# Attention and routed experts on one core: a tile's bias rows loaded by halves, two GpSimd steps made full height

## The chip, the cores and the metric

One core of a Trainium2 chip runs the whole program in one launch. The metric is the device time of one execution in microseconds, taken as the median over runs. The kernel before takes 859.41 us (three runs, 858.2 to 860.89).

## The reference

Causal attention with a learned decay feeds a top-1 mixture of experts.

```python
# q, k, v: (8, 8, 576, 64), s: (8, 8, 576)
scores = q @ k.T / sqrt(64)
cum    = cumsum(maximum(s, 0), -1)
bias   = minimum(-(cum[:, None] - cum[None, :]), 0)      # per row and column
scores = where(causal, -1e9, scores + bias)
attn   = softmax(scores) @ v                             # (8, 8, 576, 64)
x      = attn as 4608 tokens of 512
e      = argmax(x @ w_gate); g = softmax weight of e     # 8 experts
out    = g * (relu(x @ w1[e]) @ w2[e])                   # 512 -> 1024 -> 512
```

Everything is float32. The kernel computes each product from a rounded high part and a low part (high times high, high times low, low times high).

## The kernel before

**Pairs and tiles.** The 64 heads are worked in 32 pairs. A pair's queries and keys lie with one head on partitions 0 to 63 and the other on 64 to 127. The 576 query rows are four tiles of 128 for each head (g = 0 to 3), and the last 64 rows of both heads together form the *mixed* tile (g = 4, `MIX`), whose rows 0 to 63 belong to the first head and 64 to 127 to the second.

**Bias.** The row part of the bias cancels in the softmax, so only a column bias is needed. It is computed once, scaled by 8, and written to a DRAM tensor `bias` of 64 x 576. For each pair `load_b` (LB, L142) brings the first 512 columns of both heads, repeated on all 128 partitions, and `load_c` (LC, L148) brings the mixed tile's `bx`: the first head's 576 values repeated on partitions 0 to 63 and the second head's on 64 to 127. Both are issued from SyncE's queue. `causal` (M0, M2, M3, M4, L152) puts -8e9 above the diagonal, on GpSimd; M4 does the last 64 columns of `bx`, one half of the partitions at a time.

**The split.** `split` (L188) makes the high and low parts: K0 on VectorE, K1 (low part of q, into `h`) and K3 (low part of k, `kl`) on GpSimd, and K4, which copies the last 64 query columns into `qd`, a tile with one 64 x 64 block per head on its diagonal and zeros off it. K4 is two copies, one per half of the partitions. There are two `qd` tiles, used in turn, and their zeros are written at the start on ScalarE.

**The steps of a pair.** TensorE computes the scores (S0 to S3; S4 and SM are the two parts of the mixed tile, of which the first product needs `qd` and the second `kl`), transposes the exponentials (T0 to T4) and multiplies with v (AV). VectorE adds the bias and takes the row maximum (Z0 to Z4, L276), ScalarE takes the exponential (X0 to X4, L290) and moves the transposes out (C0 to C4, L320). Every four pairs form a batch of 576 tokens, whose routing (RA to RD and others; eight steps on TensorE) is spread over later pairs. Its rows are scattered by expert into a DRAM tensor `xs` by GpSimd's indirect transfers (SD, L462).

**What sets the order.** `ORDER` is a list per engine, written by hand; "+n" is how many pairs a step lags. `loop` walks the lists and emits each step as soon as the steps that it needs are emitted, so every engine runs its list strictly in order. What the change touches:

```python
"POOL": "M0+1 K1+0 M2+1 K4+0 M4+0 K3+0 SD+0 M3+0",
"SP": "PASS+3 LB+2 LV+4 LX+0 LC+1",
```

PASS is a step on SyncE that waits for S4 of its pair; SM waits for it, and so do the transfers behind it in SyncE's queue. By the lags, LC of pair p stands behind PASS of pair p-2. There are two buffers of `bx`, two of `b`, two of `kl`.

**After the attention** the experts run one after the other on the sorted tokens (L846 to L1060): two layers, with the rows written to the output by GpSimd's indirect transfers (L896).

Of the kernel before, what the change touches and what calls it, by code (L numbers as in the profile page):

```python
# [8 lines left out]
F32 = mybir.dt.float32  # L9
# [4 lines left out]
AF = mybir.ActivationFunctionType  # L14
ALU = mybir.AluOpType
# [4 lines left out]
P, HP = 128, 64  # L20
B, H, S, D = 8, 8, 576, 64
# [10 lines left out]
BIG = -8.0e9  # L32
# [44 lines left out]
class Attention:  # L77
    def __init__(self, ctx, tc, K, qkv, s, rt, ps_t, dr):
        self.tc, self.nc, self.K, self.qkv, self.rt, self.ps_t = tc, tc.nc, K, qkv, rt, ps_t
        nc = tc.nc  # L80
        pool = lambda name, bufs: ctx.enter_context(tc.tile_pool(name=name, bufs=bufs))
        self.ldx, c2, c0, self.lq, self.ld, self.ldv = (
            pool("a_x", 3), pool("a_c2", 1), pool("a_c0", 1), pool("a_q", 2), pool("a_k", 2), pool("a_v", 4),
        )
        self.wk, c1, cp, self.sm = pool("a_wk", ZB), pool("a_c1", 1), pool("a_c", 1), pool("a_sm", 10)
        self.lb, self.lc = pool("a_b", NB), pool("a_bx", NB)
        self.qd = [c2.tile([P, 2, 2, HP], F32R, name=f"qd{i}") for i in range(2)]
        self.Es = [c1.tile([P, 2, w], F32, name=f"E{g}") for g, w in enumerate(TW[:4])]
        self.Es.append(c1.tile([P, 640], F32, name="E4"))
        self.aT = [(c0, cp)[i].tile([P, 5, 2, S], F32, name=f"aT{i}") for i in range(2)]  # L90
        self.ps_s = ctx.enter_context(tc.tile_pool(name="ps_s", bufs=2, space=PSUM))
        self.st = {}
        self.open = True

        flat = self.aT[1].rearrange("p a h c -> p (a h c)")
        raw, cum, zz, rows = (flat[:, S * i : S * i + S] for i in range(4))
        self.bias = dr.tile([B * H, S], F32, name="bias")
        keep = tc.keep_in_program_order
        keep(nc.vector.memset(zz, 0.0))
        self.queue(nc.sync.dma_start(raw[: B * H], s))  # L100
        self.load(0)
        self.load(1)
        for i in range(2):
            nc.scalar.activation(
                self.qd[i].rearrange("p a h c -> p (a h c)"), zz[:, : 4 * HP], AF.Copy
            )
        self.split(0, 0)
        r = slice(0, B * H)
        keep(nc.vector.tensor_scalar(out=raw[r], in0=raw[r], scalar1=0.0, scalar2=None, op0=ALU.max))
        keep(nc.vector.tensor_tensor_scan(  # L110
            out=cum[r], data0=raw[r], data1=zz[r], initial=0.0, op0=ALU.add, op1=ALU.add
        ))
        keep(nc.vector.tensor_scalar(
            out=rows[r], in0=cum[r], scalar1=cum[r, S // 2 : S // 2 + 1], scalar2=8.0, op0=ALU.subtract, op1=ALU.mult
        ))
        for part in (1, 3):
            keep(self.split(0, part))
        self.split(0, 4)
        self.rows = rows[r]

        warm = self.ps_s.tile([P, 2, 512], F32, name="s")[:, 0]
        zb = zz.bitcast(BF16)
        for x in range(WARM):
            for c in ((0, 256), (256, 512)) if x % 3 == 0 else ((0, 512),):
                nc.tensor.matmul(
                    warm[:, c[0] : c[1]], zb[:, :P], zb[:, P + c[0] : P + c[1]],
                    start=True, stop=True, skip_group_check=True,
                )
        nc.gpsimd.memset(self.Es[MIX][:, S:], 0.0)
        self.LT = rt.tile([P, 640], F32, name="LT", bufs=1)  # L130
        nc.gpsimd.memset(self.LT[:, S:], 0.0)
        self.xb, self.sums, self.sumx, self.rr, self.ra = [], [], [], [], []
        for i in range(2):
            self.xb.append(rt.tile([P, 4, 640], F32, name=f"xb{i}", bufs=1))
            nc.gpsimd.memset(self.xb[i][:, :, S:], 0.0)
            self.sums.append(rt.tile([P, 4, 8], F32, name=f"sums{i}", bufs=1))
            self.sumx.append(rt.tile([P, 4], F32, name=f"sumx{i}", bufs=1))
            self.rr.append(rt.tile([P, 5, 8], F32, name=f"rr{i}", bufs=1))
            nc.gpsimd.memset(self.rr[i][:, 4], 1.0)
            self.ra.append(rt.tile([P, 2, 5, 4], F32, name=f"ra{i}", bufs=1))  # L140
# [6 lines left out]

    def load_c(self, p):  # L148
        x = self.st.setdefault(p, {})["c"] = self.lc.tile([P, S], F32, name="bx")
        self.queue(self.nc.sync.dma_start(x, self.bias[2 * p : 2 * p + 2].unsqueeze(1).broadcast_to([2, 64, S])))  # L150

    def causal(self, p, part):  # L152
        aff = lambda out, x, pattern: self.nc.gpsimd.affine_select(  # L153
            out=out, in_=x, pattern=pattern, compare_op=ALU.is_ge, fill=BIG, base=0, channel_multiplier=1
        )
        b = self.st[p]["b"]
        if part == 0:
            cut = lambda x: x.rearrange("p h (k c) -> p h k c", c=P)
            aff(cut(b[:, :, 512:]), cut(b[:, :, :256]), [[0, 2], [0, 2], [-1, P]])
        elif part in (2, 3):  # L160
            x = b[:, :, P * part : P * part + P]
            aff(x, x, [[0, 2], [-1, P]])
        else:
            for h in range(2):
                x = self.st[p]["c"][64 * h : 64 * h + 64, 512:]
                aff(x, x, [[-1, 64]])

    def load(self, p):
        x = self.ldx.tile([P, 2 * S], F32, name="qk")
# [18 lines left out]
    def split(self, p, part):  # L188
        nc = self.nc
        d = self.st[p]  # L190
        q, k = d["x"][:, :S], d["x"][:, S:]
        if part == 0:
            d["h"] = self.lq.tile([P, 3, S], F32R, name="h")
            d["kl"] = self.ld.tile([P, S], F32R, name="kl")
            if p:
                nc.vector.tensor_copy(d["h"][:, :2].rearrange("p a c -> p (a c)"), d["x"])
            else:
                for i, x in enumerate((q, k)):
                    nc.scalar.activation(d["h"][:, i], x, AF.Copy)
        elif part in (1, 3):  # L200
            x, hi, lo = (q, d["h"][:, 0], d["h"][:, 2]) if part == 1 else (k, d["h"][:, 1], d["kl"])
            e = nc.gpsimd if p else nc.vector
            return e.tensor_tensor(out=lo, in0=x, in1=hi.bitcast(F32), op=ALU.subtract)  # L203
        else:
            for h in range(2):
                r = slice(64 * h, 64 * h + 64)
                nc.gpsimd.tensor_copy(self.qd[p % 2][r, :, h], d["h"][r, ::2, 512:].bitcast(F32))

    def mms(self, groups, first=True, last=True):
        for n in range(len(groups[0][1])):  # L210
# [970 lines left out]
```

## Time and profile before

| what | value |
|---|---|
| median of three runs | 859.41 us (858.2 to 860.89) |
| the profiled execution | 861.1 us, its span 859.4 us |
| TensorE products busy | 768.7 us, 89% |
| weight loads busy | 616.9 us, 72% |
| VectorE busy | 448.1 us, 52% |
| ScalarE busy | 426.5 us, 50% |
| GpSimd busy | 262.2 us, 31% |
| mean granted TensorE clock | 0.945 of full speed |
| transfers | 131.59 MB, mean 153 GB/s |

The profile is of one execution. PE is TensorE (PEld its weight loads), DVE VectorE, ACT ScalarE, POOL GpSimd, SP SyncE; a q behind a name is that engine's queue of issued transfers. L153 is line 153 of the kernel. "out<-in" gives an operation's tiles by their names in the program. Where an engine sat idle before an operation, the bracket gives how long and what released it; a wait for several things is put down to the one that came last. TensorE's times are modelled at their ends, so its busy share is not a measure of its use. GpSimd's are rough.

### The profile page before, as it was taken

How to read it: one execution, taken by the hardware profiler on the slowest of the kernel's cores; microseconds unless marked ns; L12 is line 12 of the kernel's file. 1: busy time of each engine (PE TensorE's matmuls, PEld its weight loads, DVE VectorE, ACT ScalarE, POOL GpSimd, SP SyncE). 2: the span in 40 equal slices, each digit the busy share in tenths (PEclk: the TensorE clock that was granted, in tenths of full speed). 3: DMA queues.
4: the chain of work that ended last, by engine and by line, in shares of the span. 5: the costliest groups of instructions: out<-in, count | busy, mean ns of one | idle time of the engine just before them, and what ended most of it. 6: DMA issues, size and time to landing. Idle time of an engine off the chain costs nothing.

```text
span 859.4 us, 18213 instructions
## 1 busy us (share of the span) xinstructions
PE 768.7 (89%) x6948; PEld 616.9 (72%) x6948; DVE 448.1 (52%) x1188; ACT 426.5 (50%) x1029; POOL 262.2 (31%) x407
## 2 busy tenths in 40 slices
PE   5487879798888797977999999999999999999987
PEld 3375767686777675755688888888788888887876
DVE  3345666666686575765651736354255255442611
ACT  1566878777787695855241515242243234331510
POOL 2444545555665656554200010101010010000001
PEclk8578999989999998989999999999999999999999
DMA  6666545556565565454670727263054045360201
GB/s 179 209 200 204 163 145 164 197 170 210 169 210 170 182 198 153 152 171 147 227 247 25 250 88 257 88 211 119 14 192 155 14 161 190 109 223 29 68 15 50
DMA packets 56746, 131.59 MB, mean 153 GB/s; under 512 B 4527, under 2 KB 4527, under 8 KB 56624
## 3 DMA queue, kind: packets, MB, share of 16 engines
q1 hardware_dynamic: 48240, 106.34, 38.4%
q0 software_dynamic: 5936, 18.92, 6.0%
q10 hardware_dynamic: 2448, 4.74, 1.5%
q8 instruction: 73, 1.20, 0.6%
q14 instruction: 49, 0.40, 0.1%
HBM read 101.97 MB, written 28.27 MB: 152 GB/s over the span
## 4 chain that ended last, share of the span: by engine, by line
PE 42%; issue 28%; DMA 13%; POOL 7%; DVE 5%; ACT 2%; POOLq 1%; SPq 1%; another core or an unknown queue 0%; DVEq 0%
PE ph L859 13%; DMA xs<-xr,dsi 8%; PE py L889 8%; PE s L212 6%; PE t L330 5%; PE t L294 3%; DVE z L276 3%; PE ph L889 3%; POOL kl L203 2%; DMA qk<-in_qkv_dram 2%; POOL bx L153 1%; ACT E L290 1%; ACT aT L320 1%; POOL out_dram L896 1%; DMA out_dram<-y,xr 1%
## 5 line engine op out<-in xcount | busy, mean ns | idle before, releaser
L859 PE MATMUL ph<-xT,w1t 128*128 128x512 f32 x768 | 181.0, 393 | 4.3 <-DVE xT L769 2.2
L290 ACT ACTIVATE E<-z,m 128x128 f32<-128x128 f32 (+4 forms) x288 | 166.0, 579 | 36.4 <-PE t L294 14.5
L859 PEld LDWEIGHTS ph<-xT,w1t 128*128 128x128 f32 x768 | 143.8, 189 | 37.7 <-DVE xT L769 2.6
L896 POOL DMA_INDIRECT out_dram<-y,xr x39 | 37.7, 966 | 390.6 <-DVE y L895 315.2
L320 ACT COPY aT<-t 128x512 f32<-128x512 f32 (+4 forms) x160 | 108.7, 685 | 78.9 <-PE t L294 77.2
L889 PE MATMUL py<-w2t,hT 128*128 128x512 f32 x552 | 130.6, 392 | 0.0
L889 PEld LDWEIGHTS py<-w2t,hT 128*128 128x128 f32 x552 | 102.5, 188 | 21.4
L276 DVE CUSTOM_DVE_ANT_0 z<-s,b 128x512 f32<-128x512 f32 (+2 forms) x192 | 91.2, 509 | 20.9 <-POOL b L153 6.3
L212 PE MATMUL s<-h 64*128 64x256 f32 (+3 forms) x512 | 98.8, 391 | 0.9 <-DVE xr L451 0.7
L330 PE MATMUL t<-aT,v 128*64 128x64 f32 (+2 forms) x1408 | 98.5, 297 | 0.6 <-ACT aT L320 0.6
L294 PEld LDWEIGHTS t<-ident,E 64*128 64x128 f32 x1600 | 76.9, 154 | 25.1 <-ACT E L290 8.8
L861 ACT ACTIVATE hT<-ph 128x512 fp32r<-128x512 f32 x64 | 37.7, 595 | 112.5 <-PE ph L859 110.7
L294 PE MATMUL t<-ident,E 64*128 64x64 f32 x1600 | 86.6, 243 | 3.3 <-ACT aT L320 3.3
L330 PEld LDWEIGHTS t<-aT,v 128*64 128x64 f32 x1408 | 69.0, 141 | 20.3 <-ACT E L290 2.8
L864 DVE SCALAR_TENSOR_TENSOR hT<-ph,hT 128x512 fp32r<-128x512 f32 x64 | 43.7, 689 | 47.2 <-ACT hT L861 46.5
L212 PE MATMUL s<-kl,qd 64*128 64x288 f32 (+1 forms) x124 | 24.7, 384 | 48.0 <-POOL kl L203 48.0
L212 PE MATMUL s<-h,qd 64*128 64x288 f32 (+1 forms) x248 | 50.1, 378 | 13.5 <-SPq L599 7.7
L276 DVE CUSTOM_DVE_ANT_0 z<-s,bx 128x576 f32<-128x576 f32 x32 | 24.2, 756 | 71.6 <-PE s L212 31.8
L212 PEld LDWEIGHTS s<-h 64*128 64x128 f32 x512 | 57.6, 222 | 4.5 <-DVE m L276 0.9
L153 POOL TENSOR_SCALAR_AFFINE_SELECT b<-b 128x256 f32<-128x256 f32 (+1 forms) x96 | 49.1, 528 | 25.8 <-DVE m L276 24.2
L889 PE MATMUL ph<-w2t,hT 128*128 128x512 f32 x216 | 53.8, 402 | 2.2 <-issue 2.2
L895 DVE TENSOR_SCALAR y<-py,xr 128x512 f32<-128x512 f32 x26 | 19.5, 750 | 69.3 <-PE py L889 69.3
(151 smaller groups left out, 1067.6 us busy)
## 6 DMA issues: line engine op xcount, KB each, us to landing
raw<-in_w_dram SPq DMA_DIRECT2D x32, 1024.0 KB, 7.0
qk<-in_qkv_dram SPq DMA_DIRECT2D x32, 576.0 KB, 11.8
b<-bias SPq DMA_DIRECT2D x32, 512.0 KB, 9.2
v<-in_qkv_dram SPq DMA_DIRECT2D x32, 320.0 KB, 9.8
bx<-bias SPq DMA_DIRECT2D x32, 288.0 KB
xr<-xs SPq DMA_DIRECT2D x8, 1028.0 KB
xs<-blank ACTq DMA_DIRECT2D x9, 514.0 KB, 8.1
xs<-blank SPq DMA_DIRECT2D x8, 514.0 KB
```

The costliest lines, as they stand in the source:

```text
L153: aff = lambda out, x, pattern: self.nc.gpsimd.affine_select(out=out, in_=x, pattern=pattern, compare_op=ALU.is_ge, fill=BIG, base=0, chan ...
L212: ins = self.nc.tensor.matmul(out, terms[n][0], terms[n][1], start=first and n == 0, stop=last and n == len(terms) - 1, skip_group_check=True,
L276: ins = nc.vector.tensor_tensor_reduce(out=cut(z[:, :w]), in0=x, in1=bias, scale=-0.125, scalar=3.0e38, op0=ALU.add, op1=ALU.min, accum_out=m,
L290: nc.scalar.activation(out, z[:, :w], AF.Exp, bias=m, scale=-1.0, accum_out=total)
L294: self.nc.tensor.transpose(out, src[r], self.K["ident"][r, r])
L320: return self.nc.scalar.copy(o, i)
L330: nc.tensor.matmul(ps[64 * h : 64 * h + 64, bank, lo - 512 * bank : hi - 512 * bank], v[:, kt, h], self.aT[p % 2][:, kt, h, lo:hi], start= ...
L859: nc.tensor.matmul(ps, w[:, a, d, c], x[:, b, d], start=n == 0, stop=n == 11)
L861: ins = nc.scalar.activation(h[:, 0, f], ps, AF.Relu)
L864: nc.vector.scalar_tensor_tensor(out=h[:, 1, f], in0=ps, scalar=0.0, in1=h[:, 0, f].bitcast(F32), op0=ALU.max, op1=ALU.subtract)
L889: self.nc.tensor.matmul(ps, hT[:, a, f, c], w[:, b, f % 4], start=f == 0 and i == 0, stop=f == 7 and i == 2)
L896: disjoint(self.tc, "out", self.nc.gpsimd.indirect_dma_start(out=self.out, out_offset=IndirectOffsetOnAxis(ap=row[:, DM + 1 : DM + 2].bitc ...
```

## The change

The mixed tile's bias rows come in two transfers of 64 partitions instead of one of 128 whose source has an outermost dimension of 2. K4 becomes one multiply on all 128 partitions: the query columns, repeated for both diagonal places, times `half`, which is 1 on a head's own block and 0 on the other, so that the zeros are written anew each time and need no preparation. M4 becomes one addition of `last`, which holds 0 up to the diagonal and -8e9 above it in each half. `half` and `last` are made once at the start on GpSimd, and the two ScalarE operations that wrote the zeros of `qd` go.

```diff
+        self.half = c2.tile([P, 2, HP], F32, name="half")
...
-        for i in range(2):
-            nc.scalar.activation(
-                self.qd[i].rearrange("p a h c -> p (a h c)"), zz[:, : 4 * HP], AF.Copy
+        self.last = c2.tile([P, HP], F32, name="last")
+        nc.gpsimd.memset(self.last, 0.0)
+        for h in range(2):
+            x = self.last[64 * h : 64 * h + 64]
+            nc.gpsimd.affine_select(
+                out=x, in_=x, pattern=[[-1, HP]], compare_op=ALU.is_ge, fill=BIG, base=0, channel_multiplier=1
             )
+        nc.gpsimd.memset(self.half, 0.0)
+        for h in range(2):
+            nc.gpsimd.memset(self.half[64 * h : 64 * h + 64, h], 1.0)
...
-        self.queue(self.nc.sync.dma_start(x, self.bias[2 * p : 2 * p + 2].unsqueeze(1).broadcast_to([2, 64, S])))
+        for h in range(2):
+            self.queue(self.nc.sync.dma_start(
+                x[64 * h : 64 * h + 64], self.bias[2 * p + h : 2 * p + h + 1].broadcast_to([64, S])
+            ))
...
-            for h in range(2):
-                x = self.st[p]["c"][64 * h : 64 * h + 64, 512:]
-                aff(x, x, [[-1, 64]])
+            x = self.st[p]["c"][:, 512:]
+            self.nc.gpsimd.tensor_tensor(out=x, in0=x, in1=self.last, op=ALU.add)
...
-            for h in range(2):
-                r = slice(64 * h, 64 * h + 64)
-                nc.gpsimd.tensor_copy(self.qd[p % 2][r, :, h], d["h"][r, ::2, 512:].bitcast(F32))
+            nc.gpsimd.tensor_tensor(
+                out=self.qd[p % 2], in0=d["h"][:, ::2, 512:].bitcast(F32).unsqueeze(2).broadcast_to([P, 2, 2, HP]),
+                in1=self.half.unsqueeze(1).broadcast_to([P, 2, 2, HP]), op=ALU.mult,
+            )
```

## Rows read from the trace of the kernel before

**Rows 1.** Busy time by stretch (from:to, length), granted clock, DMA share, GB/s.
```profile
core 0: us, PE busy (x) PEld busy (x) DVE busy (x) ACT busy (x) POOL busy (x), PEclk, DMA share, GB/s
...
18.00:400.00 382.00, 314.30 (x4653) 254.08 (x4653) 238.81 (x834) 274.52 (x750) 209.05 (x339) 0.89 0.58 183
...
146.00:352.00 206.00, 174.32 (x2668) 142.23 (x2670) 139.04 (x484) 155.85 (x427) 124.55 (x193) 0.93 0.58 183
226.00:246.00 20.00, 19.92 (x338) 16.03 (x333) 15.98 (x57) 19.08 (x57) 11.27 (x19) 1.00 0.62 198
```

**Rows 2.** Waits in 18 to 400: total us, times, longest us.
```profile
PE s L212 <- POOL kl L203: 48.0, 24, 5.1
...
PE s L212 <- POOL qd L207: 4.7, 4, 1.5
...
POOL bx L153 <- DMA bx<-bias: 65.2, 19, 6.6
POOL qd L207 <- DMA xs<-xr,dsi: 44.4, 14, 5.0
```

**Rows 3.** Order of time: issues and masks of bx (start, us; idle before).
```profile
8.52 0.64 SPq L150 DMA_DIRECT2D bx<-bias  x1
...
106.71 0.50 SPq L150 DMA_DIRECT2D bx<-bias  x1
...
17.11 0.53 POOL L153 TENSOR_SCALAR_AFFINE_SELECT bx<-bx 64x64 f32<-64x64 f32 x2 [7.69 <-DMA bx<-bias]
...
123.48 0.52 POOL L153 TENSOR_SCALAR_AFFINE_SELECT bx<-bx 64x64 f32<-64x64 f32 x2 [3.94 <-DMA bx<-bias]
```

**Rows 4.** A stretch within the first bx transfer: busy times, then packets.
```profile
14.30:15.90 1.60, 0.00 (x0) 0.00 (x0) 0.00 (x0) 0.00 (x0) 0.00 (x0) 0.53 0.13 50
...
DMA packets 35, 0.08 MB, mean 50 GB/s; under 512 B 0, under 2 KB 0, under 8 KB 35
```

**Rows 5.** GpSimd in order of time.
```profile
27.17 1.40 POOL L203 TENSOR_TENSOR kl<-qk,h 128x576 fp32r<-128x576 f32 x1
...
149.07 0.97 POOL L462 DMA_INDIRECT xs<-xr,dsi  x1 [0.30 <-issue]
150.04 1.02 POOL L153 TENSOR_SCALAR_AFFINE_SELECT b<-b 128x256 f32<-128x256 f32 x2
...
152.75 0.28 POOL L207 CAST qd<-h 64x128 fp32r<-64x128 f32 x1
156.72 0.29 POOL L207 CAST qd<-h 64x128 fp32r<-64x128 f32 x1 [3.69 <-DMA xs<-xr,dsi]
...
350.38 1.41 POOL L203 TENSOR_TENSOR kl<-qk,h 128x576 fp32r<-128x576 f32 x1
...
367.38 1.41 POOL L203 TENSOR_TENSOR kl<-qk,h 128x576 fp32r<-128x576 f32 x1
```

**Rows 6.** The chain that ended last, its first step: the load of s.
```profile
0.82 2.87 DMA aT<-in_s_dram
```

**Rows 7.** GpSimd's operations by line and shape, 18 to 420: busy, mean ns.
```profile
L203 POOL TENSOR_TENSOR h<-qk,h 128x576 fp32r<-128x576 f32 x31 | 44.0, 1419 | 11.0 <-PE s L212 6.4 <-PE t L294 2.4 <-DVE h L196 2.1
...
L207 POOL CAST qd<-h 64x128 fp32r<-64x128 f32 x62 | 18.7, 301 | 45.4 <-DMA xs<-xr,dsi 44.4
...
L153 POOL TENSOR_SCALAR_AFFINE_SELECT bx<-bx 64x64 f32<-64x64 f32 x62 | 15.8, 256 | 67.5 <-DMA bx<-bias 65.2
...
L791 POOL TENSOR_TENSOR w1t<-raw,w1t 128x512 fp32r<-128x512 f32 x4 | 5.0, 1278 | 0.0
```

**Rows 8.** TensorE in order of time: the mixed tile's products.
```profile
159.59 0.40 PE L212 MATMUL s<-kl,qd 64*128 64x288 f32 x2 [2.13 <-POOL kl L203]
...
227.87 0.38 PE L212 MATMUL s<-h,qd 64*128 64x288 f32 x2
...
237.21 0.40 PE L212 MATMUL s<-h,qd 64*128 64x288 f32 x2
...
245.71 0.40 PE L212 MATMUL s<-h,qd 64*128 64x288 f32 x2
```

## The prediction, as put on record before the result was known

> **What bounds the kernel now.** I read the page's engine shares first, then the busy times by stretch, the waits of TensorE and GpSimd, GpSimd's work and SyncE's queue in order of time, and last a stretch in which TensorE doesn't wait.
>
> The change touches only the attention, which ends near 400 us. There no engine is full: TensorE is busy 314.30 of 382 us, ScalarE 274.52, GpSimd 209.05, at a granted TensorE clock of 0.89 [rows 1]. So the attention is held by waits. TensorE's largest is 48.0 us in 24 waits for `kl`, which GpSimd makes at L203 (K3); 4.7 us go to `qd` [rows 2]. GpSimd is free nearly half of the time, but late: it waits 65.2 us before the mixed tile's mask (L153, M4) for the `bx` transfer and 44.4 us before a `qd` cast (L207, K4), put down to scatters into `xs` [rows 2]. In its queue stand K4, M4, K3: whatever holds the first two holds `kl`, and TensorE with it.
>
> The first stall: `bx` lands late because it moves slowly. The k-th pair of masks belongs to the k-th transfer. The first was issued at 8.52 and its masks started at 17.11, the tenth at 106.71 and 123.48: 8.6 and 16.8 us [rows 3]. In 14.3 to 15.9 only 35 packets move, 0.08 MB, so 2304 bytes each: `bx` rows. The share of the 16 DMA engines is then 0.13, that is 2.1 engines, at 50 GB/s [rows 4]. At 35 packets in 1.6 us, 128 need 5.9 us with nothing beside them. Over the whole attention the engines are at 0.58 [rows 1]: most have room, while `bx` crowds a few. That closes a loop of two pairs: LC of pair p is issued behind PASS of p-2 and lands 17 us later; then come M4, K3, S4 and PASS of p.
>
> The second stall: the second of K4's two half-height casts waits 3.69 us, until 156.72, behind scatters issued until 149.07, while the masks at 150.04 and the first cast at 152.75, which stand between, don't [rows 5]. Neither `h` nor `qd` is scattered data. I read it as a wait that comes with an operation on partitions 64 to 127 alone, and expect an operation on all 128 to be free of it, as those masks are.
>
> **The change, part by part.** *The bias rows.* Each new transfer is 64 rows of 2304 bytes, as the load of `s` is, which lands in 2.87 us [rows 6]. I expect 3 to 7 us beside the others, against a need some 17 us after the issue: the mask's wait goes. SyncE issues one transfer more per pair, at about 0.5 us [rows 3]. Behind it in that queue stand the next pair's PASS and LB, nine microseconds later, so I count nothing; without that cover it is 0.5 x 30 = 15 us. The gain I price by TensorE's pace below, not by GpSimd's 65.2 us, most of which TensorE never saw.
>
> By the Trainium skill (DMA: Bandwidth & Descriptors, "Rules for kernel authors") an outermost dimension of size c below 16 confines a transfer to at most c engines; the 0.13 above, with an outermost 2, agrees. The same table says of two transfers to disjoint halves of the partitions "Don't bother", since they serialize on the same engines; no row here has such a pair, and by that rule alone the first part of the sum would be lost (rival 3).
>
> *K4.* Two casts of 301 ns become one multiply of two inputs, 128 x 256. The trace has none; the nearest rows are subtractions, 1278 ns for 128x512 and 1419 ns for 128x576 [rows 7], a slope of 2.2 ns an element, so 1278 - 256 x 2.2 gives 0.71 us. Ends: 0.30 (one cast) and 1.42 (the larger subtraction). I take 0.71, from the nearest shape: 0.1 us dearer than the casts.
>
> *M4.* Two masks of 256 ns become one addition, 128 x 64: by the same slope 1278 - 448 x 2.2 gives 0.29 us; ends 0.1 (the slope alone, nothing fixed) and 0.71. I take 0.29, 0.2 us cheaper. Together K4 and M4 are level. They have slack, too: without the stall GpSimd would have gone from the first cast at 152.75 [rows 5] through 0.60 of casts, 0.51 of masks, 1.41 of `kl` and some 0.2 between them to 155.5, and TensorE asked for `kl` at 159.59 - 2.13 = 157.46 [rows 8], 2.0 us later.
>
> *Setup.* Six small GpSimd operations come and two ScalarE activations go. Before the first bias transfer, issued at 8.52 [rows 3], GpSimd has no mask to make, which hides them; uncovered, six at about 0.25 us are 1.5 us.
>
> **The sum**, against the profiled execution: 861.1 us, its span 859.4 and 1.7 around it.
> - Pairs 1 to 29: `kl` starts at 27.17 and at 350.38 [rows 5], 323.2 us, 28 pairs at 11.54. Without waits TensorE is its own limit. In 226 to 246 it had none, at clock 1.00 [rows 1]: the mixed tile's first products start at 227.87, 237.21 and 245.71 [rows 8], so 9.34 and 8.50 us a pair, mean 8.92. These two pairs carry four of the eight routing steps of a batch of four pairs, the gate product among them, so they are no low sample. To the mean I add 0.6: ScalarE needs 155.85 / 18 = 8.7 us a pair in 146 to 352 [rows 1], near enough to hold TensorE at times, and some of the low clock (0.93 there) will stay. 9.5 us a pair gives 28 x (11.54 - 9.5) = 57 us.
> - Start: the first mask can run at 8.52 + 0.6 + 2.9 = 12.0 instead of 17.11 [rows 3], and the loads queued behind `bx` on its engines gain too. 6 us, ends 4 and 8.
> - Pairs 30 and 31 and everything behind: 0. From 350.38 to 367.38 [rows 5] two pairs already take 8.50 each.
>
> 63 us: 798.1 for an execution such as the profiled one, which stands 1.7 above the median of the three runs shown (859.41). The forecast is 796. What is late next is TensorE itself, ScalarE just behind it.
>
> **Rivals.**
> 1. *The scatter wait stays*: it hangs on something else in K4, or moves to the mask. For: its cause is inferred from where it stands. Against: the full-height masks behind scatters never show it. GpSimd then keeps 44.4 of its 109.6 us of stalls, 41%, and TensorE's pace gains 59% of 57, 34 us, with the start 40: 819 in the median.
> 2. *Another engine takes the place.* ScalarE at 8.7 us, in step with TensorE through two buffers, could hold pairs at 10.3: 28 x 1.24 + 6 = 41, so 818. For: ScalarE has no other reserve. Against: in 226 to 246 it is busy 19.08 of 20 us [rows 1] and TensorE doesn't wait for it.
> 3. *The halves don't move faster.* Landing stays near 17 us; only the scatter wait goes, and the wait for `bx` behind it takes most of that over: within 10 us of before, 852. For: they share a queue with `b`, `v` and `qk`. Against: the 2.87 us of `s` [rows 6]. The rule on halves, above, would end here.
> 4. *Slower: the multiply is dear.* It stands in front of M4 and K3. From 0.6 + 2.0 of slack + 52.7 / 28 = 1.9 of stall now, 4.5 us, it costs more than all that goes; at 5 us, 28 x 0.5 = 14, so 873. Against: no two-input row is over 1.42 us [rows 7].
>
> **How the numbers follow.** Forecast 0.70, rivals 0.12, 0.11, 0.05 and 0.02. The forecast's own ends: 9.1 us a pair and 8 at the start, 76 us, 783; 10.4 and 4, 36 us, 823. The range, 782 to 830, takes in rivals 1 and 2 and leaves out 3, 4 and the low tail. A measurement of this kernel tells 0.3% (2.6 us) from no change: faster 0.95 (forecast, rivals 1 and 2, and some of 3), within it 0.03, slower 0.02.
>
> **What would show it.** In the profile after: GpSimd's wait for `bx` under 10 us, and none for scatters before `qd`; TensorE's wait for `kl` under 10 us in all; `kl` of pair 1 near 21 and of pair 29 near 287; the multiply near 0.7 us, the addition near 0.3; a granted clock above 0.93 in the attention; the stretch from `kl` of pair 31 to the end within 2 us of its 492. The prediction is wrong if `bx` still lands 10 us or more after its issue, if TensorE waits as long for ScalarE as it did for `kl`, or if the multiply takes over 2.7 us.

## The result, and the profile after

The changed kernel takes 772.81 us (median of 4 runs, 771.24 to 775.53), the kernel before 860.07 beside it (4 runs, 858.2 to 860.89): a ratio of 0.8992, 95% interval 0.8958 to 0.9025. Forecast were 796 us and a range of 782 to 830. The direction was right, the size too small: 87 us, not 63, and below the range's low end. In some jobs both kernels run slower and the change gives less (0.9116 and 0.9098 in two later jobs, 0.8983 and 0.9000 in two others); the last section comes back to that.

The profiled execution takes 771.24 us, its span 769.5, which is 89.9 less than the span before. In the lines of the changed kernel K1 and K3 are L212, K4 is L214, M4 L175, the other masks L163, the scatters L472.

Busy times by stretch, changed kernel, columns as in [rows 1]: the attention from 18 us until shortly before its end, and four pairs, one batch, within it.

```profile
18.00:300.00 282.00, 268.93 (x4416) 219.86 (x4415) 237.14 (x814) 261.46 (x728) 196.32 (x269) 0.97 0.78 237
150.30:185.30 35.00, 34.84 (x597) 28.80 (x593) 31.38 (x109) 33.86 (x96) 26.27 (x35) 1.00 0.78 237
```

TensorE is busy 34.84 of 35 us at a granted clock of 1.00, ScalarE 33.86; before, the attention had 0.89 and no engine was full [rows 1]. The DMA share rises from 0.58 to 0.78: the same bytes in less time. TensorE's products are busy 738.2 us over the whole execution instead of 768.7, for the same products. That fits the granted clock, 0.89 before and 0.97 now: a larger part of the attention ran at 1.2 GHz instead of 2.4 before.

Waits of the changed kernel in 18 to 315, columns as in [rows 2].

```profile
POOL h L212 <- PE s L222: 40.5, 21, 3.8
ACT aT L330 <- PE t L304: 12.1, 20, 2.7
...
PE t L304 <- ACT aT L330: 4.1, 5, 1.8
POOL bx L175 <- DMA bx<-bias: 4.0, 2, 2.5
...
PE s L222 <- POOL qd L214: 1.6, 1, 1.6
...
PE s L222 <- POOL kl L212: 1.0, 1, 1.0
```

All four rows of [rows 2] are answered: TensorE's 48.0 us for `kl` are 1.0, its 4.7 for `qd` 1.6, GpSimd's 65.2 for `bx` 4.0, and the 44.4 for scatters are gone. GpSimd now waits for TensorE (40.5), so the direction has turned round.

The first two issues of `bx`, the halves of pair 0, on SyncE's queue, then GpSimd of the changed kernel in order of time: start, duration, what it did, idle time before.

```profile
8.41 1.11 SPq L158 DMA_DIRECT2D bx<-bias  x2
```
```profile
12.31 0.32 POOL L175 TENSOR_TENSOR bx<-bx,last 128x64 f32<-128x64 f32 x1 [2.13 <-DMA bx<-bias]
...
20.81 1.40 POOL L212 TENSOR_TENSOR kl<-qk,h 128x576 fp32r<-128x576 f32 x1
...
153.29 0.97 POOL L472 DMA_INDIRECT xs<-xr,dsi  x1 [0.30 <-issue]
...
157.85 0.73 POOL L214 TENSOR_TENSOR qd<-h,half 128x256 fp32r<-128x256 f32 x1
158.54 0.32 POOL L175 TENSOR_TENSOR bx<-bx,last 128x64 f32<-128x64 f32 x1
158.81 1.43 POOL L212 TENSOR_TENSOR kl<-qk,h 128x576 fp32r<-128x576 f32 x1
...
264.22 1.42 POOL L212 TENSOR_TENSOR kl<-qk,h 128x576 fp32r<-128x576 f32 x1
...
283.20 1.39 POOL L212 TENSOR_TENSOR kl<-qk,h 128x576 fp32r<-128x576 f32 x1
```

From these and [rows 5] the 89.9 us of span divide. Start: `kl` of pair 1 at 20.81 instead of 27.17, 6.4 us. Pairs 1 to 29: 243.4 us instead of 323.2, 79.8, or 8.69 a pair instead of 11.54. Pairs 30 and 31: 18.98 instead of 17.00, 2.0 lost. From `kl` of pair 31 to the end, called the tail below: 486.3 instead of 492.0, 5.7 won. What makes the last pair longer (10.35 us in the changed kernel, 8.54 before) was not followed up.

### The profile page after: what moved, and what is told of

Same layout as the page of the kernel before. It is cut to its first block, busy times and chain, and to the rows that moved or that the text cites. A ratio compares the mean times of both kernels' runs of the same rounds, so it can differ in the third digit from the quotient of the medians.

```text
span 769.5 us, 18149 instructions
## 1 busy us (share of the span) xinstructions
PE 738.2 (96%) x6948; PEld 594.8 (77%) x6948; DVE 449.9 (58%) x1188; ACT 422.0 (55%) x1027; POOL 257.3 (33%) x349
## 4 chain that ended last, share of the span: by engine, by line
PE 34%; issue 18%; DMA 8%; DVE 3%; POOL 1%; POOLq 1%; ACT 1%; another core or an unknown queue 1%; DVEq 0%
PE ph L869 14%; PE py L899 9%; DMA xs<-xr,dsi 6%; PE ph L899 3%; PE t L340 2%; DMA out_dram<-y,xr 1%; PE s L222 1%; POOL out_dram L906 1%; PE t L770 1%; PE ph L925 1%; PE t L304 1%; DMA xr<-xs 1%; DVE z L286 1%; PE ph L953 1%
## 5 line engine op out<-in xcount | busy, mean ns | idle before, releaser
L330 ACT COPY aT<-t 128x512 f32<-128x512 f32 (+4 forms) x160 | 108.1, 684 | 15.5 <-PE t L304 12.1
L222 PE MATMUL s<-h 64*128 64x256 f32 (+3 forms) x512 | 88.8, 356 | 1.1 <-DVE xr L461 0.7
L304 PEld LDWEIGHTS t<-ident,E 64*128 64x128 f32 x1600 | 69.5, 140 | 24.9 <-ACT E L300 9.6
L304 PE MATMUL t<-ident,E 64*128 64x64 f32 x1600 | 80.1, 228 | 4.1 <-ACT aT L330 4.1
L163 POOL TENSOR_SCALAR_AFFINE_SELECT b<-b 128x256 f32<-128x256 f32 (+1 forms) x96 | 49.1, 528 | 30.7 <-DVE m L286 23.2
L212 POOL TENSOR_TENSOR h<-qk,h 128x576 fp32r<-128x576 f32 x31 | 44.0, 1420 | 45.2 <-PE s L222 40.5
L300 ACT ACTIVATION_READ_ACCUMULATOR E<-z,m 128x1 f32 x288 | 55.2, 192 | 0.0
L899 PE MATMUL ph<-w2t,hT 128*128 128x512 f32 x216 | 52.2, 393 | 2.6 <-issue 2.6
L222 PEld LDWEIGHTS s<-h 64*128 64x128 f32 x512 | 50.4, 194 | 4.4 <-DVE m L286 1.3
L778 ACT ACTIVATE xT<-t 128x512 fp32r<-128x512 f32 x32 | 19.1, 598 | 62.5 <-PE t L770 55.8
```

Of the source, the lines that this page charges most:

```text
L163: aff = lambda out, x, pattern: self.nc.gpsimd.affine_select(out=out, in_=x, pattern=pattern, compare_op=ALU.is_ge, fill=BIG, base=0, chan ...
L222: ins = self.nc.tensor.matmul(out, terms[n][0], terms[n][1], start=first and n == 0, stop=last and n == len(terms) - 1, skip_group_check=True,
L300: nc.scalar.activation(out, z[:, :w], AF.Exp, bias=m, scale=-1.0, accum_out=total)
L304: self.nc.tensor.transpose(out, src[r], self.K["ident"][r, r])
L330: return self.nc.scalar.copy(o, i)
L899: self.nc.tensor.matmul(ps, hT[:, a, f, c], w[:, b, f % 4], start=f == 0 and i == 0, stop=f == 7 and i == 2)
```

## The experiments

All ratios are to the kernel before, run in the same job. A job, A to E, is a set of kernels run together on one chip; C and D have the same chip number. "Pace" is the mean distance of `kl` from pair 1 to pair 29 in the profile.

| job | kernel | ratio | 95% interval | pace, us |
|---|---|---|---|---|
| A | split_only | 0.9200 | 0.9169 to 0.9231 | 9.29 |
| A | full_only | 0.9896 | 0.9837 to 0.9956 | 11.47 |
| A | columns | 0.9957 | 0.9934 to 0.9979 | 11.50 |
| A | casts_back | 0.9110 | 0.9082 to 0.9137 | 9.24 |
| B | masks_back | 0.9137 | 0.9109 to 0.9165 | 9.27 |
| B | spare_tile | 0.9950 | 0.9918 to 0.9982 | 11.46 |
| B | sixteen | 0.9205 | 0.9177 to 0.9233 | 9.15 |
| B | after_again (the changed kernel) | 0.9116 | 0.9088 to 0.9145 | 9.18 |
| C | one_exp | 0.9013 | 0.8966 to 0.9059 | 8.83 |
| C | two_terms | 0.8916 | 0.8868 to 0.8964 | 8.62 |
| C | late_scatter | 0.8985 | 0.8944 to 0.9026 | 8.69 |
| C | after_third (the changed kernel) | 0.8983 | 0.8941 to 0.9024 | 8.69 |
| D | copy_moved | 0.9053 | 0.9012 to 0.9093 | 9.10 |
| D | copy_moved_two_terms | 0.9051 | 0.9009 to 0.9092 | 9.06 |
| D | after_fourth (the changed kernel) | 0.9098 | 0.9052 to 0.9143 | 9.13 |
| E | early_scatter | 0.9115 | 0.9089 to 0.9142 | 9.03 |
| E | copy_moved_2 | 0.9027 | 0.9000 to 0.9055 | 8.88 |
| E | after_fifth (the changed kernel) | 0.9000 | 0.8968 to 0.9032 | 8.79 |

### Which part of the change does it

**split_only**: the kernel before with this edit alone.

```diff
-        self.queue(self.nc.sync.dma_start(x, self.bias[2 * p : 2 * p + 2].unsqueeze(1).broadcast_to([2, 64, S])))
+        for h in range(2):
+            self.queue(self.nc.sync.dma_start(
+                x[64 * h : 64 * h + 64], self.bias[2 * p + h : 2 * p + h + 1].broadcast_to([64, S])
+            ))
```

> The kernel before with the bias rows in two transfers alone; the casts, the two masks and everything else as before. Theory (two stalls of different cause): `bx` lands early, GpSimd's wait for it falls from 65 us to under 10, but the second half-height cast still waits for the scatters, over 20 us in all, and TensorE still waits over 10 us for `kl`: 800 to 825 us. Rival (the scatter wait was only a part of the loop that the late `bx` closes, and goes with it): 770 to 785 us, no scatter wait over 5 us in all.

**full_only**: the change without that edit.

> The changed kernel with the bias rows in one transfer whose outermost dimension is 2, as before; the full-height multiply and addition stay. Theory: `bx` still lands 15 us or more after its issue once the loop runs, GpSimd waits over 60 us for it, and it takes over most of what the scatter wait had: 835 to 860 us. Rival (the scatter wait was the larger part): under 815 us.

**casts_back**: the change with K4 as it was.

```diff
-            nc.gpsimd.tensor_tensor(out=self.qd[p % 2], ..., op=ALU.mult)
+            for h in range(2):
+                r = slice(64 * h, 64 * h + 64)
+                nc.gpsimd.tensor_copy(self.qd[p % 2][r, :, h], d["h"][r, ::2, 512:].bitcast(F32))
```

> The changed kernel with the diagonal q blocks again made by two half-height casts (and the blocks zeroed once on ScalarE), the mask still one full-height addition. Theory (the wait for scatters comes with a GpSimd operation on partitions 64 to 127 alone): GpSimd waits over 20 us for scatters ahead of the second cast, 795 to 825 us, within 1% of the kernel with the two transfers alone. Rival (the two masks cause it too or instead): under 785 us, or well below the kernel with the two transfers alone.

**masks_back**: the change with M4 as it was.

```diff
-            x = self.st[p]["c"][:, 512:]
-            self.nc.gpsimd.tensor_tensor(out=x, in0=x, in1=self.last, op=ALU.add)
+            for h in range(2):
+                x = self.st[p]["c"][64 * h : 64 * h + 64, 512:]
+                aff(x, x, [[-1, 64]])
```

> The changed kernel with the mixed tile's mask again as two half-height operations; the diagonal q blocks stay one multiply. So far: two transfers alone 0.920 of the time before, the changed kernel with the two casts back 0.911, the changed kernel 0.899. Theory (the casts carry the cost, because TensorE's first mixed product then takes two signals of GpSimd; the masks are nearly free): 0.897 to 0.904, pairs of 8.5 to 8.6 us with one of four at 9.4. Rival (any second half-height operation of GpSimd costs the same): 0.908 to 0.915, with two pairs of four about a microsecond longer than in the changed kernel.

The waits of full_only in 18 to 400, then of split_only in 18 to 330:

```profile
POOL bx L172 <- DMA bx<-bias: 120.4, 31, 6.6
PE s L219 <- POOL kl L209: 51.2, 25, 5.6
```
```profile
POOL bx L156 <- DMA bx<-bias: 4.7, 4, 1.7
PE s L215 <- POOL kl L206: 3.3, 3, 1.9
```

In full_only the waits for scatters are gone, as the prediction said of an operation on all partitions: its multiply starts 2.7 us after the last scatter's issue has ended and waits for nothing.

```profile
149.21 0.97 POOL L469 DMA_INDIRECT xs<-xr,dsi  x1 [0.30 <-issue]
...
152.92 0.73 POOL L211 TENSOR_TENSOR qd<-h,half 128x256 fp32r<-128x256 f32 x1
```

But the wait for `bx` has grown from 65.2 to 120.4 us, more than the two had together [rows 2], and TensorE waits for `kl` as long as before. That is the prediction's third rival made real: it gave 852 us, and 0.9896 of 859.4 is 850. In split_only the theory failed: it expected over 20 us of waits for scatters and 800 to 825 us on the base of 859, and there are none, at 0.920 of the time, 791 on that base. The rival was nearer: the scatter wait belonged to the loop that the late `bx` closes. GpSimd of casts_back, in order of time, shows the same with the two casts in place:

```profile
158.79 0.97 POOL L471 DMA_INDIRECT xs<-xr,dsi  x1 [0.30 <-issue]
...
164.58 0.63 POOL L216 CAST qd<-h 64x128 fp32r<-64x128 f32 x2
```

The casts run 5.8 us after the last scatter's issue without a wait; before, the second one waited until 7.65 us after it [rows 5]. So casts_back's theory failed too: it expected over 20 us of such waits. Two things have changed. The casts come later: in the pairs with scatters 4.8 to 5.6 us after the end of the last issue (4.2 to 5.6 in split_only), where the first of the two came after 2.7 to 4.3 before, because GpSimd now waits for TensorE in between. And the scatters land sooner; that `bx` no longer crowds a few engines is the likely reason, and not shown by a run of its own. The page's row of DMA issues gives the median from issue to landing (last number), first of the kernel before, then of the changed one:

```profile
xs<-xr,dsi POOLq DMA_INDIRECT x40, 6.3
```
```profile
xs<-xr,dsi POOLq DMA_INDIRECT x40, 4.3
```

So the size of the GpSimd edits is this: the changed kernel stood at 0.9116 in job B, masks_back at 0.9137 there and casts_back at 0.911 in job A, with intervals that overlap; neither edit shows a gain of its own. (masks_back lies where its rival wanted it, but so does the changed kernel in that job, so the run decides nothing between theory and rival.) The split in two brings 0.080 in job A, where the whole change brings 0.088 in job B, and most of the rest is a matter of placement (below). Jobs A and B are both of the slower kind; what the two edits are worth in the others was not measured.

### What makes the halves fast

**columns**: two transfers again, but cut along the columns, so that each keeps an outermost dimension of 2.

```diff
-        for h in range(2):
-            ...
+        for a in range(2):
+            c = slice(288 * a, 288 * a + 288)
+            self.queue(self.nc.sync.dma_start(
+                x[:, c], self.bias[2 * p : 2 * p + 2, c].unsqueeze(1).broadcast_to([2, 64, 288])
+            ))
```

> The changed kernel with the bias rows in two transfers cut along the columns (288 each), so that each still has the outermost dimension 2 and covers all 128 partitions; the byte count is the same, packets are twice as many and half as long. Theory (the outermost dimension sets how many engines work): the DMA share while only these move stays near 0.13, GpSimd's wait for `bx` stays over 50 us, and the time is that of the kernel with one transfer or longer, 840 to 890 us. Rival (two smaller transfers instead of one is what helps): 770 to 790 us.

**sixteen**: one transfer, with an outermost dimension of 16.

```diff
+        self.wide = dr.tile([8 * B * H, S], F32, name="wide")
...
+        self.queue(self.nc.sync.dma_start(
+            self.wide.rearrange("(h x) s -> h x s", x=8), self.rows.unsqueeze(1).broadcast_to([B * H, 8, S])))
...
+        self.queue(self.nc.sync.dma_start(
+            x, self.wide[16 * p : 16 * p + 16].unsqueeze(1).broadcast_to([16, 8, S])))
```

> The changed kernel with the bias rows in one transfer of all 128 partitions again, but read from a copy in DRAM that holds every row eight times, so that its outermost dimension is 16 instead of 2 (one transfer more at the start, 1.2 MB, ahead of the first bias rows). Theory (the outermost dimension sets how many engines work, not the number of transfers): `bx` lands early, GpSimd waits under 10 us for it in all, pairs run as in the changed kernel, and only the start is later, by 3 to 8 us: ratio 0.899 to 0.910. Rival (it is the splitting in two that frees the engines): near the kernel with one transfer, 0.98 to 1.0.

First a stretch at the start of the changed kernel in which nearly only the first two halves move: busy times, then packets, as in [rows 4].

```profile
9.50:10.50 1.00, 0.66 (x6) 0.43 (x6) 0.00 (x0) 0.00 (x0) 0.68 (x5) 1.00 0.41 141
```
```profile
DMA packets 74, 0.14 MB, mean 141 GB/s; under 512 B 13, under 2 KB 13, under 8 KB 74
```

The halves move at a DMA share of 0.41 and 141 GB/s, where the one transfer had 0.13 and 50 [rows 4]. Each half reads a single row of `bias` over and over, so it wasn't the repeated reading of few rows that was slow.

Next such a stretch at the start of columns. Then its wait for `bx` in 18 to 400, and the same wait of sixteen in 18 to 330:

```profile
16.00:17.00 1.00, 0.00 (x0) 0.00 (x0) 0.00 (x0) 0.00 (x0) 0.00 (x0) 0.50 0.15 54
```
```profile
DMA packets 46, 0.05 MB, mean 54 GB/s; under 512 B 2, under 2 KB 44, under 8 KB 46
```
```profile
POOL bx L176 <- DMA bx<-bias: 125.9, 32, 7.8
```
```profile
POOL bx L175 <- DMA bx<-wide: 10.9, 3, 8.1
```

Half rows of 1152 bytes (42 of the 46 packets lie between 512 bytes and 2 KB) move at 54 GB/s and a DMA share of 0.15, as whole rows did in one transfer (50 and 0.13 [rows 4]), and the time is that of full_only. One transfer with an outermost 16 runs at the changed kernel's pace, 9.15 against 9.18 in the same job. Of its 10.9 us of waits for `bx`, 8.1 are the first one, behind the copy; for the same reason its first `kl` starts at 25.89 instead of 21.23. Its ratio, 0.9205, misses the 0.899 to 0.910 that were expected. In part that is the job (the changed kernel itself has 0.9116 there), and its median stands 7.5 us above the changed kernel's, of which the later start explains 4.7 at most: its profiled execution, the fastest of five, is only 0.3 us longer than the changed kernel's. So the outermost dimension decides, not the number of transfers. The Trainium skill (DMA: Bandwidth & Descriptors, "Rules for kernel authors") says so of an outermost size below 16, and these runs agree. Its other rule there, not to bother with two transfers to disjoint halves, is not borne out where the one transfer's outermost dimension is 2: splitting it gave 0.920.

### Where the tail's 5.7 us come from

**spare_tile**: the kernel before, with a tile that nothing reads.

```diff
+        self.last = c2.tile([P, HP], F32, name="last")
+        nc.gpsimd.memset(self.last, 0.0)
```

> The kernel before with one more constant tile of 128 x 64 beside the q blocks, set to zero once and never read: it does nothing but shift what is placed after it in SBUF. Theory (the 5.7 us that the changed kernel gains behind the last pair are a matter of placement: without the tile the first expert's weight buffer lies on the last pair's `v`, with it on rows that TensorE has read earlier): GpSimd's wait of 9.2 us for TensorE ahead of the first cast of `w1t` is gone, the stretch from the first product of expert 0 to that of expert 1 falls from 65.9 to about 61 us, and the time by 4 to 6 us, ratio 0.993 to 0.996. Rival (the tail gains from the attention's faster pace or from the higher clock before it): ratio 0.998 to 1.002, the wait stays.

GpSimd in order of time where the first expert's weights are made, before, after, and in spare_tile:

```profile
389.92 0.92 POOL L462 DMA_INDIRECT xs<-xr,dsi  x1 [0.30 <-DVE m L276]
...
400.17 1.17 POOL L790 CAST w1t<-raw 128x512 fp32r<-128x512 f32 x2 [9.16 <-PE t L330]
```
```profile
307.13 0.92 POOL L472 DMA_INDIRECT xs<-xr,dsi  x1 [0.30 <-DVE m L286]
...
308.13 1.18 POOL L800 CAST w1t<-raw 128x512 fp32r<-128x512 f32 x2
```
```profile
396.14 0.91 POOL L464 DMA_INDIRECT xs<-xr,dsi  x1 [1.93 <-DVE xr L453]
...
397.14 1.19 POOL L792 CAST w1t<-raw 128x512 fp32r<-128x512 f32 x2
```

Before, the first cast of `w1t` waits 9.16 us for the last pair's product with v (AV, L330). After, and in spare_tile, it starts as soon as the last scatter is issued. Since the tile does nothing but shift what is placed behind it, the buffer of `w1t` presumably lay on something that this product reads; whether that is `v` or the other operand, the profile doesn't say. From the first product of expert 0 to that of expert 1 it is 65.9 us before, 60.8 after and 62.1 in spare_tile (about 61 were expected). The unread tile is worth 0.5% (0.2 to 0.8), 4.3 us, the tail's gain within what can be measured. Job A has the same pair: split_only adds no tile and waits, casts_back adds `last` and doesn't, and their tails are 498.8 and 494.7 us.

```profile
341.63 1.17 POOL L793 CAST w1t<-raw 128x512 fp32r<-128x512 f32 x2 [13.73 <-PE t L333]
```
```profile
324.50 1.16 POOL L799 CAST w1t<-raw 128x512 fp32r<-128x512 f32 x2 [0.21 <-remote]
```

It has nothing to do with what the change is about: two new constants shift the placement.

### What sets the pace now

**one_exp**: ScalarE does one exponential twice. **two_terms**: TensorE leaves out the third product of the scores of groups 0 to 3.

```diff
-            nc.scalar.activation(out, z[:, :w], AF.Exp, bias=m, scale=-1.0, accum_out=total)
+            for _ in range(2 if (g, h) == (0, 0) else 1):
+                nc.scalar.activation(out, z[:, :w], AF.Exp, bias=m, scale=-1.0, accum_out=total)
```
```diff
-            groups.append((ps[:, h, :w], [(qh, kh), (qh, kl), (ql, kh)]))
+            groups.append((ps[:, h, :w], [(qh, kh), (qh, kl)]))
```

> The changed kernel with one exponential more on ScalarE in every pair: that of the first head's 128 x 128 tile is done twice, 0.59 us with the reading of its sum (0.40 + 0.19). Theory (TensorE alone sets the pace, and ScalarE, busy 8.1 us of a pair's 8.7, hides it): within 4 us of the changed kernel of this job. Rival (the prediction's surcharge of 0.6 us a pair, ScalarE in step with TensorE): 10 to 18 us slower, pairs of 9.1 us or more where the changed kernel has 8.5.

> The changed kernel without the third of the three products of the scores of groups 0 to 3 (the low half of q against k), which leaves out a part of the scores' accuracy: TensorE does 8 products less in a pair, which take 0.62 us there (0.11, 0.11, 0.17 and 0.23 from one start to the next, two heads side by side); ScalarE, VectorE and GpSimd do what they did. Theory (TensorE alone sets the pace): 12 to 18 us faster than the changed kernel of this job, until ScalarE with 8.1 us a pair takes over. Rival (ScalarE in step with TensorE, or the waits between them): under 5 us faster.

Four pairs each, `kl` to `kl`, columns as in [rows 1]: after_third, one_exp, two_terms.

```profile
150.67:185.67 35.00, 34.84 (x597) 28.89 (x594) 31.38 (x109) 33.85 (x96) 26.27 (x35) 1.00 0.77 238
```
```profile
152.47:188.02 35.55, 35.15 (x597) 28.64 (x594) 31.50 (x109) 35.16 (x104) 26.29 (x35) 1.00 0.76 236
```
```profile
149.02:183.78 34.76, 33.54 (x565) 26.40 (x562) 31.36 (x109) 33.81 (x95) 26.28 (x35) 1.00 0.81 236
```

In one_exp ScalarE's busy time grows by 1.31 us in four pairs (33.85 to 35.16; 0.59 a pair was expected). The pairs grow by 0.55, and ScalarE is then full: 35.16 of 35.55. The median is 3.2 us longer, within the theory's 4. In two_terms TensorE's busy time falls by 1.30 us in four pairs (34.84 to 33.54; 0.62 a pair was expected), and the pairs shrink by 0.24 only, with ScalarE then busy 33.81 of 34.76. The median falls by 6.8 us, which misses the theory's 12 to 18 and overshoots the rival's 5; of the 7.3 us between the two profiled spans 4.2 lie behind the last `kl`. The theory had counted 8.1 us a pair for ScalarE; the row above has 33.85 / 4 = 8.46, so there was less to be won.

A third of a microsecond a pair more on ScalarE thus costs 0.14, and as much less on TensorE gives 0.06. So the two are nearly tied, and as they stand the tie costs little. Which of them leads, and why the pairs of two_terms don't come down to ScalarE's busy time, is not shown.

**copy_moved** and **copy_moved_two_terms** move one eviction to VectorE, the second without the third product too; **copy_moved_2** is the first one again, in job E.

```diff
-EVAC = {g: "A" for g in range(5)}
+EVAC = {g: "V" if g == 0 else "A" for g in range(5)}
...
-    "DVE": "... CI+4 XB+4 RAd+4 ...",
+    "DVE": "... CI+4 XB+4 C0+3 RAd+4 ...",
...
-    "ACT": "... EI+4 C0+3 C2+3 ...",
+    "ACT": "... EI+4 C2+3 ...",
```

> The changed kernel with the eviction of the transposes of group 0 (128 x 256, about 0.4 us a pair) on VectorE instead of ScalarE. In four pairs of the changed kernel, 35.0 us, TensorE is busy 34.84, ScalarE 33.85 and VectorE 31.38. Theory (TensorE and ScalarE are tied, TensorE a little ahead): within 3 us of the changed kernel of this job, pairs of 8.5 us as before. Rival 1 (ScalarE is the one that sets the pace): 8 us or more faster. Rival 2 (VectorE or the round of waits holds it): 5 us or more slower.

> The same, and without the third product of the scores of groups 0 to 3, which leaves out a part of the scores' accuracy: 0.62 us a pair less for TensorE and about 0.4 less for ScalarE. That third product alone gave 6.8 us. Theory (a tie, so that only less of both shortens a pair): 12 to 18 us faster than the changed kernel of this job, pairs of 8.2 us, with VectorE next. Rival (a third limit holds 8.5 us): 5 to 8 us, as without the move.

> The eviction of group 0 on VectorE, once more. If it relieves ScalarE, 2 to 6 us faster than the changed kernel of this job on either kind of chip; if it only helped because of the delay, within 2 us or slower where the delay is absent.

This was meant to take the load off both tied engines, and it decides nothing: the first gained 4.1 us on the changed kernel beside it, with ratios whose intervals overlap, which is neither "within 3" nor 8, and the second no more (0.9051 and 0.9053): 4.5 us, not 12 to 18. Pairs that take 8.5 us in the changed kernel took 8.7 to 8.9 with the copy on VectorE in both, so the move put something else in TensorE's way; what it is was not found. In job E, which doesn't show the delay told of below, the moved copy is 1.9 us slower than the changed kernel, within the intervals, as the second case of its expectation has it. No version was found that is faster than the changed kernel in both kinds of jobs; two_terms, run in job C alone, leaves work out.

### The scatters and the slower jobs

**late_scatter** and **early_scatter** change GpSimd's order alone.

```diff
-    "POOL": "M0+1 K1+0 M2+1 K4+0 M4+0 K3+0 SD+0 M3+0",
+    "POOL": "M0+1 K1+0 M2+1 K4+0 M4+0 K3+0 M3+0 SD+0",     # late_scatter
+    "POOL": "M0+1 SD+0 K1+0 M2+1 K4+0 M4+0 K3+0 M3+0",     # early_scatter
```

> The changed kernel with one change in GpSimd's order: the scatters of a pair stand behind the masks of group 3 instead of ahead of them, about 1 us later. In the two later profiles of the changed kernel's family, VectorE and ScalarE took up TensorE's transposes 1.0 to 1.3 us later than in the first one in each pair with two scatters, at equal times of all that was issued before. Theory (the delay belongs to the scatters that are being issued): it moves or shrinks with them, the two long pairs of four (10.4 and 9.8 us) change by 0.5 us or more, and the time by 5 us or more. Rival (it belongs to the place in the order, whatever GpSimd does): both pairs stay within 0.2 us, the time within 3 us. Where the changed kernel of this job shows no such delay, both expect no change.

> The changed kernel with the scatters of a pair ahead of its subtraction K1 in GpSimd's order instead of behind K3, which puts them some 4 us away from the transposes that were taken up late, and K1, K4, M4 and K3 up to 2.6 us later in a pair with two scatters, against 2.0 us of slack: at most 1 us a pair lost. Theory (the delay belongs to the scatters being issued): where the changed kernel of this job shows the delay, VectorE's first multiply of the routing step starts at most 0.3 us behind the transposes, and the two long pairs of four are 0.5 us or more shorter. Rival (it belongs to the place in TensorE's order): the multiply still starts 1.1 us behind them. Without the delay on this chip: within 5 us of the changed kernel, slower if at all.

Both ran in jobs without the delay that they were to move (C and E), so they say nothing on its cause. late_scatter costs nothing. early_scatter is 9.9 us slower than the changed kernel beside it, where at most 5 were expected. The lists run strictly in order, and the scatters now wait for their row numbers (`dsi`, 22.6 us in four waits between 118 and 270 us) ahead of K1 and so of `kl`. TensorE's own waits for `kl` are 4.1 us there, so this is a part of the 9.9.

The changed kernel itself, for comparison in four of the five jobs:

> The changed kernel itself, so that the three others have it on the same chip: ratio 0.896 to 0.903.

> The changed kernel itself, so that the three others have it on the same chip: ratio 0.896 to 0.915, by whether the delay of a microsecond in the pairs with two scatters shows on this chip.

> The changed kernel itself, for the comparison on the same chip: ratio 0.896 to 0.915.

> The changed kernel itself, for the comparison on the same chip: pairs of 8.69 us without the delay, 9.15 with it.

The second and the third lie within what was expected (0.8983 and 0.9098). The first, after_again, does not: 0.9116 where at most 0.903 was expected. The fourth, with pairs of 8.79 us in the mean, lies between its two values, near the one without the delay.

## Why the prediction was wrong

- **The bound, and the first stall: right.** `bx` moved on two engines' worth of DMA, and columns and sixteen show that its outermost dimension was the reason. The first mask came at 12.31 (forecast 12.0), 3.9 us after the issue instead of 8.6, `kl` of pair 1 at 20.81 (near 21), the wait for `bx` is 4.0 us (under 10).
- **The second stall: half right, and without weight.** An operation on all partitions is free of the wait for scatters (full_only). But the wait needed no cure of its own: with `bx` early the scatters have landed when the casts come, and the two casts don't wait either (split_only, casts_back). Rival 1 rested on the same error.
- **K4 and M4: right.** The multiply takes 0.73 us (0.71 forecast) and the addition 0.32 (0.29). Together they are level; no slack was used up, and rival 4 had no ground.
- **The step that failed: "To the mean I add 0.6."** It was put there for ScalarE, which would "hold TensorE at times", and for some low clock that would stay. Hardly any of it came. The clock was 1.00 in the steady pairs and 0.97 over the attention, and TensorE's products waited 4.1 us for ScalarE's copies between 18 and 315 us, not 0.6 us a pair, with ScalarE 97% busy beside it. Even 0.33 us a pair more of ScalarE's time cost only 0.14 a pair (one_exp). In place of 9.5 us a pair the run has 8.69. From 9.50 to 8.92, the mean without the surcharge, is 0.58 us, 28 times: 16 us.
- **The mean itself was a little high.** Its two pairs, 9.34 and 8.50 us [rows 8], held one with the gate product, which is one pair of four, not of two: in after_third four pairs take 35.00 us, 8.75 each. The pace was 8.69: 28 x (8.92 - 8.69) = 6.4 us more. Together these two make the 22.6 us by which the pairs beat the forecast (79.8 against 57).
- **The tail: not foreseen.** Forecast 0 within 2, measured 5.7 less, by the placement of a buffer (spare_tile). Pairs 30 and 31, counted with it, gave 2.0 back, so this term, put at 0, came to 3.7.
- **The range.** Its low end, 782, came from 9.1 us a pair. The profile's own clean pairs had 8.92, and nothing in the rows excluded them. With the pace of 8.92 and the upper bound of the start the sum would have been 81 us, 778, still without the tail.

In job B, which has the delay, the changed kernel saves 76 us (868.16 to 792.28). That is nearer to the forecast by luck: what takes the time there is not what the prediction charged.

## What to carry to other kernels

Where one transfer feeds an in-order queue, read its DMA share with nothing beside it before its bytes: 0.13 of 16 engines pointed to the cause here, a source with an outermost dimension of 2. When a stall goes, take the pace of the stretch that already runs without it, over one whole period of the schedule, and charge a near-tie of two engines only where a row shows one holding the other. Ask of every new tile what it moves in memory, and see whether a second wait on the same queue is a stall of its own before curing it.

## What the runs showed of the hardware

The changed kernel's pace was 8.69 us a pair in the first profile and in job C and 8.79 in job E, but 9.18 and 9.13 in jobs B and D. In B and D the pairs run as in the others until the first one with two scatters; from there on two pairs of four, those with two scatters, take 10.4 and 9.7 to 9.8 us instead of 9.4 and 8.5. (casts_back and split_only show the same in job A.) That it goes by the chip is not shown: jobs C and D have the same chip number. Nor is it all in those pairs: from `kl` of pair 31 to the first product of expert 0 it is 42.3 and 41.1 us in B and D, but 35.5, 36.3 and 36.0 in the first profile, C and E. The kernel before is slower in the same jobs (868.71, 868.16 and 868.62 us in A, B and D, 861.96 and 861.44 in C and E), while the kernels with slow `bx` that were profiled there keep the old pace (11.46 to 11.50, against 11.54). So the pairs lose time to the delay only once `bx` doesn't hold them, and the change gives less there.

TensorE's and VectorE's rows in such a pair, changed kernel, first profile, then job B:

```profile
152.39 0.48 PE L304 MATMUL s<-ident,LT 64*128 64x64 f32 x10
```
```profile
152.33 0.76 DVE L329 COPY xb<-t 128x576 f32<-128x576 f32 x1 [0.97 <-PE t L340]
153.01 0.55 DVE L396 TENSOR_TENSOR part<-s,ra 128x160 f32<-128x160 f32 x2
```
```profile
157.67 0.47 PE L304 MATMUL s<-ident,LT 64*128 64x64 f32 x10
```
```profile
157.61 0.76 DVE L329 COPY xb<-t 128x576 f32<-128x576 f32 x1 [0.97 <-issue]
159.32 0.56 DVE L396 TENSOR_TENSOR part<-s,ra 128x160 f32<-128x160 f32 x2 [0.95 <-PE t L304]
```

In both the copy starts 0.06 us before the transposes. The multiply that reads the transposes starts 0.62 us after their start in the first and 1.65 in the second, though the program is the same and TensorE's row for them is as long (0.48 and 0.47). Scatters are being issued in that moment in both. Whether the delay comes from them was not settled, and what differs between the jobs is not known.
